# Cross-shaped window attention: x loaded by transposing DMAs, and VectorE's share of the exponentials made from bit fields

## The chip, the cores and the metric

One Trainium2 chip; the program runs on one core. The time is device microseconds of one execution. The kernel before takes 1147.38 us (median of three runs, 1147.14 to 1147.86). The profile comes from another, profiled execution, which took 1150.81 us.

## The reference

`x` is an image of 224 x 224 tokens with 96 channels, bf16. It is projected to q, k and v, each of 96 channels. The first 48 channels attend inside horizontal strips of 8 rows (28 strips of 1792 tokens), the last 48 inside vertical strips of 8 columns (again 28 strips of 1792). Each strip is a full softmax attention of 1792 queries over 1792 keys; the two halves are joined and projected by `wo`.

```python
qkv = jnp.einsum('bhwc,cd->bhwd', x, wqkv)        # C = 96, then q, k, v of 96 channels
scale = C2 ** (-0.5)                              # C2 = 48
# h half: 8 whole rows per strip; v half: 8 whole columns per strip
ah = _softmax(jnp.einsum('bqc,bkc->bqk', qh, kh) * scale, axis=-1)
oh = jnp.einsum('bqk,bkc->bqc', ah, vh)
...
return jnp.einsum('bhwc,cd->bhwd', o, wo)         # o = [oh, ov] along the channels
```

## The kernel before, in words

**Work.** Two strips make a pair (P); 14 horizontal pairs are followed by 14 vertical ones, 28 in all. The two strips of a pair, w = 0 and 1, lie in the two halves of the 128 partitions. A pair has four query chunks (`CH`: 512, 512, 512 and 256 queries). A unit is one key tile of 128 keys against a 512-query chunk, for both strips, or two key tiles against the 256-query chunk: 14 + 14 + 14 + 7 = 49 units per pair, 1372 in all. A unit's scores are 128 x 1024 fp32 in PSUM (two banks).

**Two kinds of unit.** An A unit (`add_a`): QK product on TensorE (L762), exponential on ScalarE from PSUM to a bf16 tile PT (L780), PV product on TensorE (L745) with V_sb as weights. A D unit (`add_d`) has its exponential made by VectorE: L804 scales the scores into an fp16 tile Y_sb; four passes of L814 (J = 4) add a constant each and write int16, whose bits read as bf16 are four shifted piecewise linear powers of two; four PV products (L745 with L_sb and VD_sb) sum them, with V scaled by four weights. GpSimd makes those scaled copies VD_sb (L610). `NDC` says how many units of each chunk are D units: 2, 2, 2 and 1, so 7 of 49.

**Preparation of a pair** (`prep`): x is loaded with tokens in partitions (x_sb, L422); TensorE transposes it against an identity (L538, four groups per pair) and VectorE copies the result from PSUM to xT_sb, channels in partitions (L526, L532); then come the K projection (four groups) with VectorE's copy and row sum (L565) and GpSimd's subtraction of the mean key (L576), the Q projection (four groups, copied by VectorE at L561), and V (four groups, L597, copied at L602). TensorE does such a group in a borrowed PSUM bank; I call it a fill. The results of a chunk leave PSUM at L709, are multiplied by `wo` (L637, L666; seven or eight more fills per pair), divided by the softmax sum (L625, L644, L673) and, in the vertical half, added on GpSimd (L677) and stored (L686).

**What sets the order.** The kernel has its own planner. Each operation is given an engine, a cost, its dependencies and the buffers it takes; the planner simulates the engines and writes out one fixed order per engine. On the chip each engine runs that order, with semaphore waits, whatever its real times are. Preparation of pair P+1 is spread over pair P by `pace`; loads of pair P+2 are put in SP's stream during pair P. PSUM holds a ring of three double banks for scores and fills, and two banks for outputs. All DMAs, loads of x and stores of the result, go through SP's one queue.

Of the kernel before, what the change touches and what calls it, by code (L numbers as in the profile page):

```python
# [8 lines left out]
FP16 = mybir.dt.float16  # L9
FP32 = mybir.dt.float32  # L10
I16 = mybir.dt.int16
# [9 lines left out]
J = 4  # L21


def _bf16(v):
    import struct
    u = struct.unpack("<I", struct.pack("<f", v))[0]
    u = (u + ((u >> 16) & 1) + 0x7FFF) & 0xFFFF0000
    return struct.unpack("<f", struct.pack("<I", u))[0]


def _spline():
    def lin(z):
        n = int(z // 1)
        return (1 + z - n) * 2.0 ** n
    a = [2.0 ** (-j / J) / J for j in range(J)]
    r = [sum(a[j] * lin(i / 4096 + j / J) for j in range(J)) / 2 ** (i / 4096) for i in range(4096)]
    mid = (max(r) + min(r)) / 2
    w = [_bf16(v) for v in a]
    return w, [-log2(J * v * mid) for v in w]


SPL_W, SPL_S = _spline()
Y_MIN = -16000.0


NDC = [2, 2, 2, 1]
DKT = 2
# [198 lines left out]
def bass_standalone__window_attn_cswin__vision_kernel(  # L246
# [19 lines left out]
    TH, FTH = 112, 8  # L266
    RPF = FTH * TH // W
# [3 lines left out]
    NPT, NY, NL, NR = 8, 2, 3, 4  # L271

    es = ExitStack()
    with es:
# [5 lines left out]
        ident = sb("ident", [128, 128], BF16)  # L280
        ident_f = sb("ident_f", [128, 128], FP32)
# [3 lines left out]
        x_sb = [sb(f"x_sb{i}", [128, 2, 16, C], BF16) for i in range(2)]  # L285
# [4 lines left out]
        VD_sb = [sb(f"VD_sb{i}", [128, J, 2, DKT, CP], BF16) for i in range(2)]  # L290
        PT = [sb(f"PT{i}", [128, 1024], BF16) for i in range(NPT)]
        Y_sb = [sb(f"Y_sb{i}", [128, 1024], FP16) for i in range(NY)]
        L_sb = [sb(f"L_sb{i}", [128, J, 1024], I16) for i in range(NL)]
# [21 lines left out]
        s_x = [[[sem(f"s_x{b}{w}{hf}") for hf in range(2)] for w in range(2)] for b in range(2)]  # L315
# [70 lines left out]
        for v in range(2):  # L386
            for w in range(2):
                o_wov0 = first("dve", 0.15, lambda e, v=v, w=w: e.memset(wo_sb[v][w][:], 0.0))
        o_one = first("dve", 0.1, lambda e: e.memset(one_sb[:], 1.0))
        o_iota = first("pool", 0.3, lambda e: e.iota(ident_f[:], [[1, 128]], base=0, channel_multiplier=-1,  # L390
                                                     allow_small_or_imprecise_dtypes=True))
        o_ident = first("dve", 0.2, lambda e: e.tensor_single_scalar(ident[:], ident_f[:], 0.0, ALU.is_equal), [o_iota])
# [8 lines left out]
        x_flat = x[0].rearrange("h w c -> (h w) c")  # L401
        x_vtiles = x[0].rearrange("(kt hh) (j dw) c -> j kt hh dw c", hh=16, dw=8)
# [4 lines left out]
        t_pe = {P: [] for P in range(NP)}  # L407

        def load(P, stream):
            b = P % 2  # L410
            for w in range(2):
                src = x_flat[(2 * P + w) * NTOK:(2 * P + w + 1) * NTOK, :].rearrange("(k p) c -> p k c", p=TH) if is_h[P] else None
                for hf in range(2):
                    sm = s_x[b][w][hf]
                    own = x_tot.get((b, w, hf), 0)
                    if is_h[P]:
                        todo = [(x_sb[b][0:TH, w, hf * FTH:(hf + 1) * FTH, :], src[:, hf * FTH:(hf + 1) * FTH, :])]
                    else:
                        todo = [(x_sb[b][:, w, kt, :], x_vtiles[2 * (P - NPH) + w, kt])
                                for kt in range(8 * hf, min(NKT, 8 * hf + 8))]  # L420
                    for i, (dst, s_) in enumerate(todo):
                        op = Op("sp", 0.06, 2.2, lambda e, dst=dst, s_=s_: e.dma_start(dst, s_),  # L422
                                t_pe[P - 2] if P >= 2 and i == 0 else [], dma=(sm, own if i == 0 else 0))
                        stream.append(op)
                        x_op[(P, w, hf)] = op
                        x_tot[(b, w, hf)] = x_tot.get((b, w, hf), 0) + 16

        load(0, q_first["sp"])
        op_w0 = Op("sp", 0.7, 2.8, lambda e: e.dma_start(w_sb[0:64, :, 0:C2], wqkv.rearrange("c (s d) -> c s d", s=6)[0:64]), [o_w0], dma=(s_w0, 0))
        q_first["sp"].insert(1, op_w0)  # L430
        op_w0 = Op("sp", 0.7, 2.8, lambda e: e.dma_start(w_sb[96:128, :, 0:C2], wqkv.rearrange("c (s d) -> c s d", s=6)[64:96]), [o_w0], dma=(s_w0, 0))
        q_first["sp"].insert(2, op_w0)
# [30 lines left out]
        for P in range(NP):  # L463
            for c in range(NCH):
                k = Chunk()
                k.P, k.c, k.bank, k.last, k.evac = P, c, None, None, None
                n = NKT if CH[c][1] == 512 else NKT // 2
                k.left = (n - NDC[c]) + J * NDC[c]
                k.begun = False
                chunks[(P, c)] = k  # L470
        q_ready, k_ready, v_ready, vd_ready = {}, {}, {}, {}
# [32 lines left out]
        def prep(P, pace=None, startup=False):  # L504
# [7 lines left out]
            xt_w = {}  # L512
            qk_war = last_qk[prev2] if prev2 >= 0 else []
            pv_war = last_pv[prev2] if prev2 >= 0 else []
            xt_war = xt_read.get(prev2, [])
            xt_read[P] = []
            for w in range(2):
                for hf in range(2):
                    if is_h[P]:
                        tp, nt = TH, FTH  # L520
                        ks = [hf * FTH + j for j in range(FTH)]

                        def ev_fn(e, bk, op, w=w, hf=hf):
                            src = bk.bitcast(BF16)[:, 0:FTH * TH].rearrange("c (r bc dw) -> c r bc dw", r=RPF, dw=8)
                            dst = xT_sb[b][:, w, :].rearrange("c (bc r dw) -> c r bc dw", r=SW, dw=8)[:, hf * RPF:(hf + 1) * RPF, :, :]
                            return e.tensor_copy(dst, src)  # L526
                    else:
                        ks = list(range(8 * hf, min(NKT, 8 * hf + 8)))
                        tp, nt = 128, len(ks)

                        def ev_fn(e, bk, op, w=w, ks=ks):
                            return e.tensor_copy(xT_sb[b][:, w, ks[0] * 128:(ks[-1] + 1) * 128], bk.bitcast(BF16)[:, 0:len(ks) * 128])  # L532

                    def pe_fn(e, bk, w=w, ks=ks, tp=tp):
                        bkb = bk.bitcast(BF16)
                        for j, k in enumerate(ks):
                            for h in range(2):
                                ins = e.transpose(bkb[64 * h:64 * h + 64, j * tp:(j + 1) * tp], x_sb[b][0:tp, w, k, 32 * h:32 * h + 64],  # L538
                                                  ident[0:tp, 0:tp])
                        return ins  # L540
                    p, ops = fill(0.055 * nt, pe_fn, [x_op[(P, w, hf)], o_ident],
                                  [("dve", 0.07 + nt * tp / 1920, ev_fn, xt_war, True, dve_ev, [], None)], soft() + xt_war)
                    t_pe[P].append(p)
                    xt_w.setdefault(w, []).append(ops[0])
            xt_all = xt_w[0] + xt_w[1]
            prevk = []
            for kind in "kq":
                for c, (q0, qs) in enumerate(CH):
                    def pe_fn(e, bk, kind=kind, q0=q0, qs=qs):
                        for w in range(2):  # L550
                            ins = e.matmul(bk[64 * w:64 * w + 64, 0:qs], lhsT=w_sb[:, wblk(P, kind), :],  # L551
                                           rhs=xT_sb[b][:, w, q0:q0 + qs], start=True, stop=True)
                        return ins
                    if kind == "q":
                        if startup:
                            def ev_fn(e, bk, op, q0=q0, qs=qs):
                                return e.activation(QT_sb[b][:, q0:q0 + qs], bk[:, 0:qs], ACTF.Copy)
                            evs = [("act", 0.55, ev_fn, qk_war, True, q_first["act"], [], None)]
                        else:
                            def ev_fn(e, bk, op, q0=q0, qs=qs):  # L560
                                return e.tensor_copy(QT_sb[b][:, q0:q0 + qs], bk[:, 0:qs])  # L561
# [20 lines left out]
                    if kind == "q":  # L582
                        q_ready[(P, c)] = ops[0]
                    else:
                        prevk.append(ops[0])
                        if c == NCH - 1:
                            k_ready[P] = ops[-1]
            v_evs = []
            for w in range(2):
                for k0 in range(0, NKT, VS):  # L590
                    n = min(VS, NKT - k0)

                    def pe_fn(e, bk, w=w, k0=k0, n=n):
                        for j in range(n):
                            for h in range(2):
                                t0 = (k0 + j) * 128 + 64 * h
                                ins = e.matmul(bk[64 * h:64 * h + 64, j * C2:(j + 1) * C2], lhsT=xT_sb[b][:, w, t0:t0 + 64],  # L597
                                               rhs=w_sb[:, wblk(P, "v"), 0:C2], start=True, stop=True)
# [4 lines left out]
                    p, ops = fill(0.045 * n, pe_fn, xt_w[w] + [op_w0, o_v1],  # L603
# [4 lines left out]
            vd_ready[P] = []  # L608
            for j in range(J):
                op = Op("pool", 0.1 + 0.001 * 2 * DKT * CP, 0.15 + 0.001 * 2 * DKT * CP, lambda e, j=j: e.tensor_scalar(  # L610
                    VD_sb[b][:, j, :, :, :], V_sb[b][:, :, 0:DKT, :], SPL_W[j], 1.0, ALU.mult, ALU.mult), v_evs + pv_war)
# [308 lines left out]
```

## Time and profile before

| quantity | value | where |
|---|---|---|
| median of three runs | 1147.38 us | times |
| the profiled execution | 1150.81 us | times |
| its span, first to last instruction | 1149.0 us | page |
| outside the span | 1.8 us | difference |
| first exponential of the main loop starts | 14.93 us | timeline, ACT |
| last one ends | 1140.8 us | timeline, ACT |
| busy: PE, ACT, DVE, POOL | 1109.8, 1094.7, 977.8, 198.3 us | page |
| granted TensorE clock, whole span | 0.991 | cores |

A row of a group reads: line, engine, operation, output tile <- input tiles, shapes, count, then busy time and mean duration of one, then the idle time of that engine just ahead of these instructions and what ended it. Busy times of successive instructions that overlap are counted once, so 1176 exponentials of 1085 ns on average are 1091.2 us busy. A row of the timeline merges neighbours of one kind: start, length, count. PE's ends are modelled, so that its busy time overstates how full it is.

### The profile page before, as it was taken

The page shows a single profiled execution, that of the slowest core. Times are in us where ns is not written, and L with a number is a line of the kernel's source. Part 1 is how long each engine was busy: PE and PEld are TensorE (multiplying, and loading weights), DVE is VectorE, ACT ScalarE, POOL GpSimd, SP SyncE. Part 2 cuts the span into 40 slices and gives each one's busy share as a digit, 9 for nine tenths or more (in the row PEclk, how much of TensorE's full clock was granted, in tenths as well). Part 3 has the DMA queues.
Part 4 walks back from the last instruction along what each step waited for, and adds up shares of the span by engine and source line. Part 5 has one row for each costly group of instructions (what it writes and reads, how often), then busy time and mean ns, then how long its engine had stood idle before and what let it go on. Part 6 is the DMA issues. An engine that isn't in the chain of part 4 may idle for free.

```text
span 1149.0 us, 30551 instructions
## 1 busy us (share of the span) xinstructions
PE 1109.8 (97%) x12888; PEld 459.3 (40%) x12888; DVE 977.8 (85%) x2138; ACT 1094.7 (95%) x1182; POOL 198.3 (17%) x256
## 2 busy tenths in 40 slices
PE   8999999999999999999999999999999999999996
PEld 3434433443443344344434433433443443344342
DVE  6898888798888978888888888898889988988974
ACT  5999999999999999999999999999999999999997
POOL 0101010010101001010112222222222313222121
PEclk7999999999999999999999999999999999999998
DMA  4011011101100110110111221121122212210011
GB/s 87 15 25 26 4 23 25 26 2 25 26 18 10 26 26 2 25 22 12 19 30 29 38 35 32 36 38 35 32 37 37 36 32 38 36 31 19 19 20 24
DMA packets 164977, 31.00 MB, mean 27 GB/s; under 512 B 164840, under 2 KB 164840, under 8 KB 164840
## 3 DMA queue, kind: packets, MB, share of 16 engines
q1 hardware_dynamic: 164840, 29.05, 13.8%
q8 instruction: 101, 1.65, 0.6%
q14 instruction: 36, 0.29, 0.1%
HBM read 19.36 MB, written 9.63 MB: 25 GB/s over the span
## 4 chain that ended last, share of the span: by engine, by line
PE 53%; DVE 25%; ACT 19%; issue 2%; DMA 0%; SPq 0%; ACTq 0%; POOL 0%; POOLq 0%
PE ps L745 24%; PE ps L762 19%; ACT PT L780 19%; DVE L_sb L814 10%; DVE Y_sb L804 7%; PE ps L538 4%; PE ps L551 3%; DVE OT_sb L709 2%; DVE KT_sb L565 2%; DVE tmp L673 2%; PE ps L597 2%; PE ps L637 1%; DVE QT_sb L561 1%; DVE V_sb L602 1%; PE ps L666 1%
## 5 line engine op out<-in xcount | busy, mean ns | idle before, releaser
L780 ACT ACTIVATE PT<-ps 128x1024 bf16<-128x1024 f32 x1176 | 1091.2, 1085 | 36.1 <-PE ps L762 26.1
L762 PE MATMUL ps<-QT_sb,KT_sb 48*128 48x512 bf16 (+1 forms) x3136 | 458.2, 357 | 8.5 <-DVE V_sb L602 1.7
L745 PE MATMUL ps<-PT,V_sb 128*64 128x512 bf16 (+1 forms) x2688 | 388.3, 360 | 0.7 <-ACT PT L780 0.7
L814 DVE TENSOR_SCALAR L_sb<-Y_sb 128x1024 int16<-128x1024 f16 x784 | 351.1, 486 | 0.7
L804 DVE TENSOR_SCALAR Y_sb<-ps 128x1024 f16<-128x1024 f32 x196 | 239.2, 1221 | 60.2 <-PE ps L762 58.2
L745 PE MATMUL ps<-L_sb,VD_sb 128*64 128x512 bf16 (+1 forms) x1792 | 270.8, 363 | 18.0 <-DVE L_sb L814 15.1
L762 PEld LDWEIGHTS ps<-QT_sb,KT_sb 48*128 48x128 bf16 x3136 | 122.0, 93 | 292.9 <-ACT PT L780 175.5
L745 PEld LDWEIGHTS ps<-PT,V_sb 128*64 128x64 bf16 x2688 | 126.9, 109 | 127.0 <-issue 104.0
L677 POOL TENSOR_TENSOR out_sb<-tmp,Ph_sb 128x384 bf16<-128x384 f32 (+1 forms) x112 | 95.5, 863 | 341.8 <-DVE tmp L673 286.5
L745 PEld LDWEIGHTS ps<-L_sb,VD_sb 128*64 128x64 bf16 x1792 | 85.5, 108 | 135.8 <-DVE L_sb L814 75.5
L576 POOL TENSOR_SCALAR KT_sb<-KT_sb,negmean 128x1792 bf16<-128x1792 bf16 x27 | 51.2, 1895 | 342.0 <-DVE rc L625 114.2
L610 POOL TENSOR_SCALAR VD_sb<-V_sb 128x256 bf16<-128x256 bf16 x112 | 51.4, 459 | 261.3 <-DVE V_sb L602 254.6
L709 DVE CAST OT_sb<-ps 128x512 bf16<-128x512 f32 x112 | 69.0, 616 | 28.7 <-PE ps L745 28.5
L551 PE MATMUL ps<-xT_sb,w_sb 128*64 128x512 bf16 x448 | 81.3, 374 | 1.1 <-DVE xT_sb L526 0.7
L565 DVE TENSOR_SCALAR_CACHE_REDUCE KT_sb<-ps 128x512 bf16<-128x512 f32 x112 | 67.7, 617 | 8.1 <-PE ps L551 7.7
L561 DVE CAST QT_sb<-ps 128x512 bf16<-128x512 f32 x108 | 66.4, 614 | 4.6 <-PE ps L551 4.6
L538 PE MATMUL ps<-ident,x_sb 112*64 112x112 bf16 (+1 forms) x1680 | 63.3, 219 | 2.4 <-DMA x_sb<-in_x_dram 1.1
L602 DVE CAST V_sb<-ps 128x480 bf16<-128x480 f32 x112 | 55.4, 500 | 10.7 <-PE ps L597 10.0
L538 PEld LDWEIGHTS ps<-ident,x_sb 112*64 112x64 bf16 (+1 forms) x1680 | 50.8, 111 | 28.1 <-issue 24.8
L673 DVE TENSOR_TENSOR tmp<-ps,rc 128x384 f32<-128x384 f32 (+1 forms) x112 | 56.3, 502 | 2.1 <-DVE rc L625 0.2
L625 DVE RECIPROCAL rc<-ps 128x4 f32<-128x4 f32 (+1 forms) x210 | 36.2, 172 | 23.2 <-PE ps L666 11.8
L644 DVE TENSOR_TENSOR Ph_sb<-ps,rc 128x384 bf16<-128x384 f32 x98 | 54.2, 553 | 1.9
(31 smaller groups left out, 315.0 us busy)
## 6 DMA issues: line engine op xcount, KB each, us to landing
x_sb<-in_x_dram SPq DMA_DIRECT2D x56, 168.0 KB, 3.5
x_sb<-in_x_dram SPq DMA_DIRECT2D x392, 24.0 KB, 2.2
out_dram<-out_sb SPq DMA_DIRECT2D x392, 24.0 KB, 1.9
wo_sb<-in_wo_dram SPq DMA_DIRECT2D x4, 9.0 KB
wo_sb<-one_sb SPq DMA_DIRECT2D x4, 0.0 KB
w_sb<-in_wqkv_dram SPq DMA_DIRECT2D x1, 36.0 KB, 2.5
w_sb<-in_wqkv_dram SPq DMA_DIRECT2D x1, 18.0 KB, 2.3
```

The costliest lines, as they stand in the source:

```text
L538: ins = e.transpose(bkb[64 * h:64 * h + 64, j * tp:(j + 1) * tp], x_sb[b][0:tp, w, k, 32 * h:32 * h + 64], ident[0:tp, 0:tp])
L551: ins = e.matmul(bk[64 * w:64 * w + 64, 0:qs], lhsT=w_sb[:, wblk(P, kind), :], rhs=xT_sb[b][:, w, q0:q0 + qs], start=True, stop=True)
L561: return e.tensor_copy(QT_sb[b][:, q0:q0 + qs], bk[:, 0:qs])
L565: return e.tensor_scalar(KT_sb[b][:, q0:q0 + qs], bk[:, 0:qs], 1.0, None, ALU.mult, ALU.add, accum_out=ksum[b][:, c:c + 1])
L673: return e.tensor_tensor(tmp[op.tok["t"]][:, 0:n, :], bk[:, 0:n * (C + 1)].rearrange("p (s c) -> p s c", s=n)[:, :, 0:C], r[:, 0:n].unsque ...
L677: return e.tensor_tensor(out_sb[b][:, w, g[0]:g[0] + n, :], tmp[hold[1].tok["t"]][:, 0:n, :], Ph_sb[:, g[0]:g[0] + n, j, :], ALU.add)
L709: return e.tensor_copy(OT_sb[b][:, q0:q0 + qs], bk[:, 0:qs])
L745: ins = e.matmul(bank(k.bank)[64 * w:64 * w + 64, 0:qs], lhsT=lhs(w, kt), rhs=rhs(w, i, qs), start=(op.tok["first"] and i == 0), stop=(k.l ...
L762: ins = e.matmul(bank(2 * s + w)[:, i * qs:(i + 1) * qs], lhsT=KT_sb[b][64 * w:64 * w + C2, kt * 128:(kt + 1) * 128], rhs=QT_sb[b][64 * w: ...
L780: a.fn = lambda e: e.activation(PT[a.tok["p"]][:].rearrange("p (s n) -> p s n", s=2), two(q.tok["s"]), ACTF.Exp, scale=scale)
L804: d.fn = lambda e: e.tensor_scalar(Y_sb[d.tok["y"]][:, :].rearrange("p (s n) -> p s n", s=2), two(q.tok["s"]), A128, Y_MIN, ALU.mult, ALU.max)
L814: t.fn = lambda e, j=j: e.tensor_scalar(L_sb[hold["l"].tok["l"]][:, j, :], Y_sb[d.tok["y"]][:, :], 127.0 * 128.0 + 128.0 * SPL_S[j], None, ...
```

## The change

1. **x.** The tile x_sb, the identity, the TensorE transposes and VectorE's copies of them go. xT_sb is written by DMA transposes on SP: each reads n tokens of 128 channels (96 and the first 32 of the next token; rows 96 to 127 of the result are not used) and writes 128 x n. A horizontal strip is one such DMA of 1792 tokens, a vertical strip eight of 224, one for each column. The last tokens of the image are loaded by a plain DMA in 2-byte pieces (two DMAs of 96 x 16 elements in all). Tokens of a strip now lie in row order (or column order for vertical strips); keys and values stay in that order, and Q is put back into the old order by VectorE's copy, which now writes with a stride, in four pieces of 448. All chunks of a pair wait for the last of the four. wqkv is loaded by one DMA ahead of the first x.
2. **VectorE's exponential.** Q carries the factor `A128`, so that PSUM holds scores in units of 1/128 of a power of two (ScalarE undoes it with `scale=LN128`). A D unit adds a constant and clamps, PSUM to int16 (I_sb). Two bitwise passes over I_sb make U_sb (mantissa bits under a fixed exponent) and E_sb (exponent bits, a power of two); one product of two tensors, I_sb and U_sb read as bf16, makes G_sb. Two PV products, of E_sb and of G_sb, both with V_sb, take the place of four. GpSimd's scaled copies go.
3. **Shares.** `NDC` is 2, 2, 2, 2: eight units of 49 are D units. Four L-type buffers in place of three. `pace` spreads 12 fills over the pair in place of 16.

In the built programs, ScalarE has 1148 exponentials (1176 before), SP's queue 252 transposing DMAs in place of 448 loads of x, and GpSimd no scaled copies.

```diff
-NDC = [2, 2, 2, 1]
-DKT = 2
+NDC = [2, 2, 2, 2]
...
-                    if is_h[P]:
-                        todo = [(x_sb[b][0:TH, w, hf * FTH:(hf + 1) * FTH, :], src[:, hf * FTH:(hf + 1) * FTH, :])]
...
+                runs = [(j * NTOK, 1, NTOK, 0)] if is_h[P] else [(j * SW + dw, W, H, dw * H) for dw in range(SW)]
...
+                    todo.append((True, xT_sb[b][:, w:w + 1, at:at + n], rows(t0, step, n, 128)))
+                for i, (tr, dst, s_) in enumerate(todo):
+                    fn = (lambda e, dst=dst, s_=s_: e.dma_start_transpose(dst, s_)) if tr else \
+                         (lambda e, dst=dst, s_=s_: e.dma_start(dst, s_, allow_slow_non_contiguous=True))
+                    op = Op("sp", 0.06, 4.0, fn, xt_read.get(P - 2, []) if i == 0 else [], dma=(s_x[b][w], own if i == 0 else 0))
...
-                        for j, k in enumerate(ks):
-                            for h in range(2):
-                                ins = e.transpose(bkb[64 * h:64 * h + 64, j * tp:(j + 1) * tp], x_sb[b][0:tp, w, k, 32 * h:32 * h + 64],
-                                                  ident[0:tp, 0:tp])
...
+                                    dst = QT_sb[b][:, :].rearrange("p (bc r dw) -> p r bc dw", r=SW, dw=8)[:, r * c:r * c + r]
+                                    src = bk[:, 0:QC].rearrange("p (r bc dw) -> p r bc dw", r=r, dw=8)
...
+                                    dst = QT_sb[b][:, :].rearrange("p (h dw) -> p dw h", dw=SW)[:, d * c:d * c + d]
+                                    src = bk[:, 0:QC].rearrange("p (dw h) -> p dw h", dw=d)
+                                return e.tensor_scalar(dst, src, A128, None, ALU.mult)
...
-            d.fn = lambda e: e.tensor_scalar(Y_sb[d.tok["y"]][:, :].rearrange("p (s n) -> p s n", s=2), two(q.tok["s"]),
-                                             A128, Y_MIN, ALU.mult, ALU.max)
+            d.fn = lambda e: e.tensor_scalar(I_sb[d.tok["y"]][:, :].rearrange("p (s n) -> p s n", s=2), two(q.tok["s"]),
+                                             128.0 * ONE, 0.0, ALU.add, ALU.max)
...
-            for j in range(J):
-                t = Op("dve", 0.334, 0.415, None, [d], [], [(ls, "l", 1)] if j == 0 else [])
...
+            f = Op("dve", 0.334, 0.415, None, [d])
+            f.fn = lambda e: e.tensor_scalar(U_sb[d.tok["y"]][:, :], I_sb[d.tok["y"]][:, :], M_FRAC, HALF, ALU.bitwise_and, ALU.bitwise_or)
+            x2 = Op("dve", 0.334, 0.415, None, [d], [], [(ls, "l", 1)])
+            x2.fn = lambda e: e.tensor_scalar(E_sb[x2.tok["l"]][:, :], I_sb[d.tok["y"]][:, :], M_EXP, E_LOW, ALU.bitwise_and, ALU.bitwise_or)
+            g = Op("dve", 0.60, 0.68, None, [f, x2], [], [], lambda op: ys.free(d.tok["y"], [op]))
+            g.fn = lambda e: e.tensor_tensor(G_sb[x2.tok["l"]][:, :], I_sb[d.tok["y"]][:, :].bitcast(BF16), U_sb[d.tok["y"]][:, :].bitcast(BF16), ALU.mult)
+            dve_ts.extend([f, x2, g])
+            for t, buf in ((x2, E_sb), (g, G_sb)):
...
-                prep(P + 1, pace=lambda n, base=base: [act_of[base + int(n * NA * PACE / 16)]])
+                prep(P + 1, pace=lambda n, base=base: [act_of[base + int(n * NA * PACE / 12)]])
```

## The prediction

> **What bounds the kernel now.** I read the split of the span by windows first: before the first exponential, the main loop, and after the last.
>
> ```profile
> 0.00:14.93 14.93, 11.46 (x148) 5.88 (x148) 8.87 (x31) 3.45 (x7) 0.44 (x5) 0.78 0.60 111
> 14.93:1140.80 1125.87, 1097.36 (x12730) 452.90 (x12728) 967.55 (x2102) 1091.15 (x1176) 196.77 (x249) 1.00 0.14 26
> 1140.80:1149.00 8.20, 0.95 (x12) 0.49 (x12) 1.38 (x5) 0.07 (x1) 1.05 (x2) 0.55 0.19 36
> ```
>
> Columns: stretch, its us, then busy us of PE, PEld, DVE, ACT and POOL, granted clock, DMA share, GB/s. The main loop is 1125.87 of 1149.0 us and ScalarE is busy in 1091.15 of it. PE looks as full, but its ends are modelled, so the waits decide:
>
> ```profile
> POOL out_sb L677 <- DVE tmp L673: 286.5, 58, 9.9
> ...
> PEld ps L762 <- ACT PT L780: 175.5, 517, 0.6
> ...
> PEld ps L745 <- DVE L_sb L814: 75.5, 209, 1.2
> ...
> ACT PT L780 <- PE ps L762: 26.1, 60, 1.4
> ```
>
> Columns: total us, times, longest. The weight loads of QK stand still 175.5 us because ScalarE has not freed a score buffer; ScalarE waits for QK 26.1 us. So ScalarE paces the loop, and PE, DVE and the fixed order only open gaps in it. ScalarE's pace and the gaps are in its own timeline (start, length, count):
>
> ```profile
> 350.52 3.77 ACT L780 ACTIVATE PT<-ps 128x1024 bf16<-128x1024 f32 x4 [0.49 <-PE ps L762]
> ...
> 754.91 1.02 ACT L780 ACTIVATE PT<-ps 128x1024 bf16<-128x1024 f32 x1 [0.81 <-PE ps L762]
> 756.17 1.94 ACT L780 ACTIVATE PT<-ps 128x1024 bf16<-128x1024 f32 x2 [0.24 <-PE ps L762]
> ```
>
> Four in a row take 3.77 us and a single one 1.02, so one follows another after (3.77 - 1.02) / 3 = 0.917 us. 1176 x 0.917 = 1078.4 us; the loop's other 47.5 us are gaps like the 0.81 and 0.24 shown, 1.7 us per pair. So the execution is 14.9 (head) + 1078.4 + 47.5 + 8.2 (tail) + 1.8 (outside the span) = 1150.8. That profiled execution is 3.4 us above the median.
>
> The rows the change touches, from the groups by line (busy us, mean ns | idle before):
>
> ```profile
> L780 ACT ACTIVATE PT<-ps 128x1024 bf16<-128x1024 f32 x1176 | 1091.2, 1085 | 36.1 <-PE ps L762 26.1 <-PE ps L745 8.8
> L814 DVE TENSOR_SCALAR L_sb<-Y_sb 128x1024 int16<-128x1024 f16 x784 | 351.1, 486 | 0.7
> L804 DVE TENSOR_SCALAR Y_sb<-ps 128x1024 f16<-128x1024 f32 x196 | 239.2, 1221 | 60.2 <-PE ps L762 58.2
> ...
> L526 DVE COPY xT_sb<-ps 128x896 bf16<-128x896 bf16 x56 | 34.1, 619 | 15.3 <-PE ps L538 15.2
> L532 DVE COPY xT_sb<-ps 128x1024 bf16<-128x1024 bf16 x28 | 19.1, 681 | 0.0
> L532 DVE COPY xT_sb<-ps 128x768 bf16<-128x768 bf16 x28 | 15.5, 553 | 8.7 <-PE ps L538 8.7
> ```
>
> **ScalarE.** One unit of 49 leaves it in every pair: 28 x 0.917 = 25.7 us, all on the path. 1148 x 0.917 = 1052.7 us. The other factor in `scale` costs nothing: same instruction, same shapes.
>
> **TensorE.** The transposes go: 63.3 us busy (L538, 1680 in the page). D's PV products fall from 28 x 7 x 4 = 784 unit passes to 28 x 8 x 2 = 448; at 270.8 / 784 = 0.345 us that is -116.1. A's PV loses one unit of 42: 388.3 / 42 = -9.2. QK is the same. PE's busy time goes from 1109.8 to 921 us, a factor of 0.83. PE is not the bound, so this shows only in the gaps. Fills per pair fall from 12 + 4 + 7.5 = 23.5 to 19.5, again 0.83. I let the gaps shrink by both: 47.5 x 0.83 x 0.83 = 32.7 us. Ends: 10 us (nearly all were collisions with fills and D's PV) and 47.5 (VectorE's chain or the fixed order makes them, not PE's load).
>
> **VectorE.** Out: 351.1 + 239.2 + 34.1 + 19.1 + 15.5 = 659.0, which leaves 977.8 - 659.0 = 318.8 us. In: 224 passes PSUM to int16, shape and sides as L804, at 239.2 / 196 = 1.22: 273.3 us. Then 448 bitwise passes and 224 products, which the trace does not have. A bitwise pass has one 2-byte source and a 2-byte result in SBUF, like L814: 351.1 / 784 = 0.448 us. Its other end is one element per cycle, L804's 1.22. I take 0.448, same shape and same kind of instruction: 200.7 us. The product of two bf16 tiles lies between the same ends; nearest is the 2-byte copy of 1024 elements that does not reach L814's rate, 0.681 (L532): 152.5 us. Sum: 318.8 + 273.3 + 200.7 + 152.5 = 945.3 us, or 86% of a span of about 1108, against 85% now. So VectorE stays beside ScalarE, at nothing. The cover is 15% wide: a product at 1.22 adds 121 us (96%), bitwise passes at 1.22 add 346 (over the span).
>
> The Trainium skill ("VectorE: DVE Perf Modes", "The perf-mode tier table") gives a product of two 16-bit tiles half the rate of a one-source pass; this fits the value taken, and the sum by it is the same.
>
> The copy of Q writes with a stride now, 1792 elements per pair as before (66.4 us, L561). L526 already writes 2-byte runs of 8 with gaps, 896 elements in 0.619 us, without a loss against L532's dense 1024 in 0.681. I cost it at nothing; if every strided write took twice as long it would be 66 us on VectorE, 92% full. All chunks of a pair wait for its last Q piece. That is the eighth of 12 paced fills, at about 0.9 x 8/12 = 0.6 of the pair ahead, some 15 us early: nothing.
>
> **GpSimd.** 51.4 us of VD_sb go; D's PV then waits for V itself. GpSimd is 17% busy, so nothing.
>
> **The load of x.** Before, the first K product starts at 9.19 us: x lands at 4.7 to 7.9, then transposes and copies. After, it starts when both strips of pair 0 have landed, and pair 1's first K product stands in PE's order right behind the first four QK products (two units), waiting for pair 1's strips, with all QK queued behind it. Let t be a strip's time through SP and the DMA engines; wqkv is issued first, at about 1.4 us for 0.67. K then starts near 2.1 + 2t + 2, the 2 being a landing (2.2 us in the page). The near row: half a strip by plain rows is one DMA, and seven took 5.25 us of SP's queue, 0.75 each, landing after 3.5. So t is at least 1.5 and K starts near 7 to 8.6. The far row: the queue's 164840 packets took 13.8% of 16 engines' 1149 us, 15.4 ns each; if every 32-byte piece (16 tokens of one channel) cost a packet, a strip is 14336 x 15.4 / 16 = 13.8 us. Then K starts at 31.7 instead of 9.2 (+22.5), and pair 1's strips land near 59 while PE reaches that product near 38 (+21): +44 us. After that a pair needs 27.6 us of DMA in a pair of some 39, loaded a pair ahead: hidden. I take the near row: with t = 2.5 K starts at 9.1, head unchanged. In the steady state SP issues at most 16 transposes per pair where it issues 28 loads now (28 in 18.7 us), behind the same waits; stores queue behind them as they do behind loads. The 2-byte DMA (1536 pieces, 1.5 us at 15.4 ns over 16 engines) is prefetched too. Tail: unchanged, 8.2.
>
> One rule speaks against this part. "VectorE: DVE Perf Modes", "The three transpose paths", gives 390 ns for a 128 x 128 transpose on TensorE and 1309 ns by DMA. This trace has only the TensorE side (63.3 us busy for 28 x 28 squares, 81 ns each); no run here shows the DMA's. If 1309 ns held for each of a strip's 14 squares in turn, t would be 18.3 us, an estimate from that page, and the sum about 1107 + 62.
>
> **Sum.** 14.9 + 1052.7 + 32.7 + 8.2 + 1.8 = 1110.3 for a profiled execution; less 3.4: 1107 us.
>
> **Rivals.**
> (a) The gaps stay, or VectorE becomes co-critical. For it: DVE waits for QK 58.2 us already and D's PV waits for L814 75.5 us; E and G must come in time, and an order written for one cost stalls in sequence if a pass is longer. Against: two PV passes wait per D unit instead of four. Gaps of 47.5 give 1122; a product at 1.22 makes VectorE 1067 us busy, and with about 70 us of unavoidable waiting (its 60.2 at L804 and the ends) 1137.
> (b) The gaps nearly vanish: 10 us give 1084.
> (c) Transposing DMAs are slow: t = 13.8 gives 1107 + 44 = 1151; from a t of 18 to 19 (two strips per pair of 39 us) every pair would wait too.
> (d) The slower one: bitwise passes at one element per cycle. VectorE is then 1291 us busy, the bound; with the head before its first D pass (15 us) about 1305, slower by 14%. It decides once bitwise passes and products average over (1085 - 318.8 - 273.3) / 672 = 0.73 us, 1085 being the loop as forecast; I took 0.53. For it: no bitwise pass is in the trace. Against: L814's integer result did not slow it.
>
> **Chances.** Forecast, 1095 to 1118: 0.50. (a), to 1145: 0.17. (b): 0.09. (c): 0.13, of which 0.03 ends within 0.2% of 1147.4 (what a measurement of this kernel can tell from no change) and 0.10 above. (d): 0.11. Faster 0.76, same 0.03, slower 0.21. The range 1082 to 1151 takes in all but (d), the upper part of (c), and a little of (b).
>
> **What would show it.** Right: 1148 exponentials with runs at 0.917, gaps near 33 us, first exponential near 15 us; E and U passes near 0.45 us and G near 0.68; VectorE about 945 us busy; PE near 921. Wrong: PE waiting for DMA xT_sb in the first 60 us or in every pair; bitwise passes of 1.2 us; ScalarE waiting for PV or QK more often than now while PE waits for G_sb.

## The result, and the profile after

The changed kernel takes 1210.11 us (median of four runs, 1207.2 to 1217.32) beside 1147.62 us for the kernel before on the same chip: ratio 1.0553, 95% interval [1.0503, 1.0602]. It is slower by 62 us where 1107 was forecast. The profiled execution took 1211.87 us, its span 1210.1.

The rows of the groups by line that answer to those shown of before:

```profile
L736 ACT ACTIVATE PT<-ps 128x1024 bf16<-128x1024 f32 x1148 | 1071.0, 1092 | 117.3 <-PE ps L718 115.4
L760 DVE TENSOR_SCALAR I_sb<-ps 128x1024 int16<-128x1024 f32 x224 | 276.0, 1232 | 47.9 <-PE ps L718 44.1
L770 DVE TENSOR_TENSOR G_sb<-I_sb,U_sb 128x1024 bf16<-128x1024 bf16 x224 | 182.0, 812 | 3.0
L521 DVE TENSOR_SCALAR QT_sb<-ps 128x448 bf16<-128x448 f32 x108 | 151.5, 1423 | 37.0 <-PE ps L504 37.0
L766 DVE TENSOR_SCALAR U_sb<-I_sb 128x1024 int16<-128x1024 int16 x224 | 97.6, 436 | 2.4
L768 DVE TENSOR_SCALAR E_sb<-I_sb 128x1024 int16<-128x1024 int16 x224 | 92.6, 413 | 0.0
```

ScalarE's own work is as forecast: 1148 exponentials. What is new stands behind the second bar: 115.4 us of waiting for QK (L718), where it was 26.1. The new exponential's passes are near their forecasts, its product (0.812 us for 0.68) less so. One row is far off: the copy of Q, 1.423 us on average where 0.62 was taken. A mean over two forms hides the size, so next comes the spread of that line's instructions (minimum, median, maximum in ns):

```profile
L521 DVE TENSOR_SCALAR QT_sb<-ps x108: 611/2130/2366, 32.3 to 1141.6; 128x448 bf16<-128x448 f32 x108
```

The 52 copies of horizontal pairs, which write runs of 8 elements, take 0.62 us each; the 56 of vertical pairs, which write single elements 16 bytes apart, take 2.13 to 2.37, 2.17 on average. The windows of one horizontal pair and two vertical ones (columns as before: us, busy PE, PEld, DVE, ACT, POOL, clock, DMA share, GB/s) show where the time is:

```profile
300.00:338.00 38.00, 36.73 (x376) 13.84 (x375) 33.57 (x69) 37.79 (x42) 2.17 (x1) 1.00 0.16 26
791.80:837.80 46.00, 39.19 (x378) 13.91 (x374) 41.06 (x70) 38.67 (x42) 9.34 (x10) 0.93 0.18 35
742.30:791.80 49.50, 45.68 (x378) 15.81 (x372) 39.44 (x72) 38.90 (x42) 8.83 (x10) 0.76 0.19 36
```

A horizontal pair takes 38.0 us, with ScalarE busy in 37.8 of it. A vertical pair, which differs by GpSimd's additions and the stores, takes 44.0 to 49.5 us, VectorE busy 6 to 7.5 us longer and the TensorE clock below full. None of these engines is full in such a pair, so the loss is in the order. The timeline of after inside one of them:

```profile
712.77 1.02 POOL L633 TENSOR_TENSOR out_sb<-tmp,Ph_sb 128x384 bf16<-128x384 f32 x1 [5.96 <-DVE tmp L629]
713.06 1.28 DVE L770 TENSOR_TENSOR G_sb<-I_sb,U_sb 128x1024 bf16<-128x1024 bf16 x1
...
714.35 4.14 DVE L521 TENSOR_SCALAR QT_sb<-ps 128x448 bf16<-128x448 f32 x2
...
716.56 0.36 PE L622 MATMUL ps<-wo_sb,OT_sb 128*64 128x97 bf16 x8 [0.70 <-DVE QT_sb L521]
716.85 0.39 PE L718 MATMUL ps<-QT_sb,KT_sb 48*128 48x512 bf16 x2
717.29 1.02 ACT L736 ACTIVATE PT<-ps 128x1024 bf16<-128x1024 f32 x1 [1.99 <-PE ps L718]
718.12 0.37 DVE L581 RECIPROCAL rc<-ps 128x4 f32<-128x4 f32 x1
718.55 0.61 PE L718 MATMUL ps<-QT_sb,KT_sb 48*128 48x512 bf16 x2 [1.30 <-DVE rc L581]
```

Two copies of Q hold VectorE for 4.14 us. The output product L622 needs the PSUM bank that the first of them empties; QK (L718) stands behind L622 in TensorE's fixed order, and ScalarE starves for 1.99 us. The next stop is 1.30 us, for a reciprocal that sat behind the second copy. Over the whole kernel TensorE's weight loads wait 49.7 us for this copy (total us, times, longest):

```profile
PEld ps L504 <- DVE QT_sb L521: 20.1, 13, 1.8
PEld ps L718 <- DVE QT_sb L521: 19.8, 24, 1.7
...
PEld ps L622 <- DVE QT_sb L521: 9.8, 6, 1.9
```

### The profile page after: what moved, and what is told of

Read it like the earlier page. It is cut to its first block, busy times and chain, and to the rows that moved or that the text cites. A ratio compares the mean times of both kernels' runs of the same rounds, so it can differ in the third digit from the quotient of the medians.

```text
span 1210.1 us, 24996 instructions
## 1 busy us (share of the span) xinstructions
PE 1096.9 (91%) x10424; PEld 399.7 (33%) x10424; DVE 1033.1 (85%) x1941; ACT 1074.4 (89%) x1154; POOL 156.2 (13%) x143
## 4 chain that ended last, share of the span: by engine, by line
DVE 39%; ACT 31%; PE 26%; issue 3%; POOL 1%; DMA 0%; POOLq 0%; SPq 0%
ACT PT L736 31%; PE ps L701 11%; PE ps L718 11%; DVE I_sb L760 11%; DVE QT_sb L521 9%; DVE G_sb L770 6%; DVE E_sb L768 3%; DVE U_sb L766 2%; DVE KT_sb L525 2%; DVE OT_sb L665 2%; DVE tmp L629 1%; PE ps L504 1%; PE ps L593 1%; PE ps L560 1%; DVE rc L581 1%
## 5 line engine op out<-in xcount | busy, mean ns | idle before, releaser
L736 ACT ACTIVATE PT<-ps 128x1024 bf16<-128x1024 f32 x1148 | 1071.0, 1092 | 117.3 <-PE ps L718 115.4
L718 PE MATMUL ps<-QT_sb,KT_sb 48*128 48x512 bf16 (+1 forms) x3136 | 512.0, 374 | 63.2 <-ACT PT L736 16.8
L701 PE MATMUL ps<-PT,V_sb 128*64 128x512 bf16 (+1 forms) x2576 | 467.4, 387 | 0.8 <-ACT PT L736 0.3
L760 DVE TENSOR_SCALAR I_sb<-ps 128x1024 int16<-128x1024 f32 x224 | 276.0, 1232 | 47.9 <-PE ps L718 44.1
L718 PEld LDWEIGHTS ps<-QT_sb,KT_sb 48*128 48x128 bf16 x3136 | 127.2, 94 | 388.9 <-ACT PT L736 184.4
L770 DVE TENSOR_TENSOR G_sb<-I_sb,U_sb 128x1024 bf16<-128x1024 bf16 x224 | 182.0, 812 | 3.0
L521 DVE TENSOR_SCALAR QT_sb<-ps 128x448 bf16<-128x448 f32 x108 | 151.5, 1423 | 37.0 <-PE ps L504 37.0
L504 PE MATMUL ps<-xT_sb,w_sb 96*64 96x512 bf16 (+1 forms) x448 | 86.2, 387 | 19.9 <-DVE QT_sb L521 14.9
L766 DVE TENSOR_SCALAR U_sb<-I_sb 128x1024 int16<-128x1024 int16 x224 | 97.6, 436 | 2.4
L701 PE MATMUL ps<-G_sb,V_sb 128*64 128x512 bf16 (+1 forms) x560 | 94.3, 367 | 5.4 <-DVE G_sb L770 4.9
L701 PE MATMUL ps<-E_sb,V_sb 128*64 128x512 bf16 (+1 forms) x560 | 93.9, 365 | 0.5 <-DVE E_sb L768 0.3
L768 DVE TENSOR_SCALAR E_sb<-I_sb 128x1024 int16<-128x1024 int16 x224 | 92.6, 413 | 0.0
L622 PE MATMUL ps<-wo_sb,OT_sb 128*64 128x97 bf16 x784 | 38.3, 222 | 14.4 <-DVE QT_sb L521 7.5
```

The lines of the kernel that those rows point to most:

```text
L504: ins = e.matmul(bk[64 * w:64 * w + 64, 0:qs], lhsT=w_sb[0:C, wblk(P, kind), :], rhs=rhs, start=True, stop=True)
L521: return e.tensor_scalar(dst, src, A128, None, ALU.mult)
L701: ins = e.matmul(bank(k.bank)[64 * w:64 * w + 64, 0:qs], lhsT=lhs(w, kt), rhs=rhs(w, i, qs), start=(op.tok["first"] and i == 0), stop=(k.l ...
L718: ins = e.matmul(bank(2 * s + w)[:, i * qs:(i + 1) * qs], lhsT=KT_sb[b][64 * w:64 * w + C2, kt * 128:(kt + 1) * 128], rhs=QT_sb[b][64 * w: ...
L736: a.fn = lambda e: e.activation(PT[a.tok["p"]][:].rearrange("p (s n) -> p s n", s=2), two(q.tok["s"]), ACTF.Exp, scale=LN128)
L760: d.fn = lambda e: e.tensor_scalar(I_sb[d.tok["y"]][:, :].rearrange("p (s n) -> p s n", s=2), two(q.tok["s"]), 128.0 * ONE, 0.0, ALU.add, ...
```

## The experiments

Theory 1: the single 2-byte writes of the vertical copy of Q are the loss. Theory 2: eight units in 49 overload VectorE beside GpSimd's additions in the vertical half. Theory 3: the short transposing DMAs of vertical pairs are the loss.

**Dense write.** All kernels are given as edits of the changed one. This one leaves the reordering of Q out, so it is no repair. (The copies in question are 56; the 52 below is the number of the horizontal ones.)

```diff
-    dst = QT_sb[b][:, :].rearrange("p (h dw) -> p dw h", dw=SW)[:, d * c:d * c + d]
+    dst = QT_sb[b][:, QC * c:QC * c + QC].rearrange("p (dw h) -> p dw h", dw=d)
```

> Vertical pairs: VectorE's copy of Q writes dense, so Q and with it the result stay in column order (the reordering is left out); every instruction and every order is as in the changed kernel, only these 52 destinations differ. Theory 1 (the 2-byte writes at a step of 16 bytes cost VectorE 2.15 us instead of 0.62, and the fixed order turns that into gaps on ScalarE and a colder TensorE): the copy takes about 0.62, vertical pairs fall from some 46 to 38-39 us, the granted clock of the second half returns to 1.00, the span is about 1095 to 1105 us. Theory 2 (eight units in 49 overload VectorE beside GpSimd's adds in the vertical half): the span falls only by the 52 x 1.5 = 80 us of copies at most, and gaps of several us per pair stay, 1140 or more. Theory 3 (the eight short transposing DMAs per strip hold up the vertical half): no change, about 1205.

Measured: 1108.66 us (one run). The groups by line:

```profile
L736 ACT ACTIVATE PT<-ps 128x1024 bf16<-128x1024 f32 x1148 | 1061.0, 1098 | 24.3 <-PE ps L718 23.5
L521 DVE TENSOR_SCALAR QT_sb<-ps 128x448 bf16<-128x448 f32 x108 | 66.3, 618 | 27.2 <-PE ps L504 26.9
```

Same instructions, order and waits; the copies cost 66.3 us, the figure the prediction used, and ScalarE's wait for QK falls from 115.4 to 23.5. Theory 1 stands. Theory 2 falls: with the same eight units the time is far below its 1140.

**Reordering inside TensorE's operand.** The Q projection reads its moving operand in the final order; VectorE copies densely.

```diff
+    rhs = xT_sb[b][0:C, w, :].rearrange("c (dw h) -> c h dw", dw=SW)[:, q0 // 8:(q0 + qs) // 8, :]
...
+    return e.tensor_scalar(QT_sb[b][:, q0:q0 + qs], bk[:, 0:qs], A128, None, ALU.mult)
```

> Vertical pairs: the Q projection itself reads x in the old order, its moving operand stepping 224 elements between neighbours, in chunks of 512 and 256; VectorE then copies dense. Theory 1: about 1095 to 1110 us if TensorE reads with that step at full rate; if it takes four times as long (some 1.2 us more per group of two products, four groups in each of 14 pairs) PE still has the room, and it stays below 1125. Theories 2 and 3: 1140 or more, 1205.

Measured: 1114.74 us, ratio to before 0.9713 [0.9698, 0.9727]. The stride costs TensorE instead: the two 512-wide products of a Q group take 1.02 to 1.04 us together, where those of K, whose operand is dense, take 0.38 to 0.41. Vertical pairs take 39.5 us.

**Reordering on the reading side.** The same elements, with the stride where VectorE reads PSUM; the operand keeps runs of 64, the write is dense.

```diff
+    rhs = xT_sb[b][0:C, w, :].rearrange("c (dw h) -> c dw h", dw=SW)[:, :, q0 // 8:(q0 + qs) // 8]
...
+    return e.tensor_scalar(QT_sb[b][:, q0:q0 + qs].rearrange("p (h dw) -> p h dw", dw=SW),
+                           bk[:, 0:qs].rearrange("p (dw h) -> p h dw", dw=SW), A128, None, ALU.mult)
```

> Vertical pairs: the Q projection reads runs of 64 tokens of each of the eight columns, and VectorE's copy reads PSUM with a step of 64 fp32 elements and writes dense. Theory 1 in its narrow form (it is the stepped write that is slow): the copy takes about 0.68 for 512 elements and the kernel about 1095 to 1105 us. If any stepping of a two-dimensional pattern is slow, the copy takes over 2 us here too and the kernel stays above 1190.

Measured: 1104.19 us, ratio 0.9629 [0.9607, 0.9651]. It computes all of the reference, so it is the change's gain without the stride's price. Vertical pairs take about 37.75 us, but two take 43.9 and 44.3; I call such pairs late pairs, and they come up again below.

**One DMA per strip.** A vertical pair loads 1792 consecutive tokens by one transposing DMA; gathering the columns is left out, so the tokens are the wrong ones. The strided write stays.

```diff
-    runs = [...] if is_h[P] else [(j * SW + dw, W, H, dw * H) for dw in range(SW)]
+    runs = [(j * NTOK, 1, NTOK, 0)]
```

> Vertical pairs load 1792 consecutive tokens by one transposing DMA per strip, as horizontal pairs do (wrong tokens: the gathering of columns is left out); Q's stepped copy stays. Theory 3: vertical pairs fall to 38-40 us, span about 1100. Theories 1 and 2: within 10 us of the changed kernel, 1200 to 1215.

Measured: 1207.58 us (one run), vertical pairs 44 to 48 us. Theory 3 falls.

**The price by itself.** A program with nothing but VectorE's copies (and two forms on ScalarE), six of each.

> Computes nothing of the reference (it writes zeros): VectorE alone, six copies of 448 elements each, one after the other, on a line for each form; ScalarE afterwards with two forms. Theory 1 (the price is that of a 2-byte write alone in its 16 bytes, on VectorE, whatever else runs): dense 0.6 to 0.7 us, runs of 8 the same, the changed kernel's vertical form 2.1 to 2.2 us, bf16 at a step of 8, 16 and 32 elements 2.1 to 2.2 as well, step 2 and 4 somewhere between; from SBUF instead of PSUM the same price as from PSUM. Rival A (the price comes from what runs beside it in the kernel, GpSimd or the DMAs): the vertical form 0.6 to 0.8 here. Rival B (the price is that of reading PSUM in two halves, not of the write): step 8 with a plain read stays at 0.6 to 0.7. Open between sub-theories: fp32 at a step of 16 bytes is 0.6 if only writes of under 4 bytes pay, 2.1 if any write alone in its 16 bytes pays; pairs (4 bytes at a 16-byte step) cost half of the single ones, 1.1, if the price is one write slot per 16 bytes touched.

Measured, in the groups by line (L93 is ScalarE, one bf16 every 16 bytes; L58 VectorE the same; L52 the changed kernel's vertical form; L56 one bf16 every 8 bytes, L54 every 4; L64 two neighbours every 16 bytes; L74 a strided read of PSUM with a dense write; L48 dense on both sides; L50 runs of 8):

```profile
L93 ACT ACTIVATE d<-ps 128x448 bf16<-128x448 f32 x6 | 12.9, 2148 | 0.2
L58 DVE TENSOR_SCALAR d<-ps 128x448 bf16<-128x448 f32 x6 | 12.8, 2136 | 0.2
L52 DVE TENSOR_SCALAR d<-ps 128x448 bf16<-128x448 f32 x6 | 12.8, 2136 | 0.2
...
L56 DVE TENSOR_SCALAR d<-ps 128x448 bf16<-128x448 f32 x6 | 6.9, 1148 | 0.2
...
L54 DVE TENSOR_SCALAR d<-ps 128x448 bf16<-128x448 f32 x6 | 3.9, 656 | 0.2
L64 DVE TENSOR_SCALAR d<-ps 128x448 bf16<-128x448 f32 x6 | 3.7, 624 | 0.2
L74 DVE TENSOR_SCALAR d<-ps 128x448 bf16<-128x448 f32 x6 | 3.7, 624 | 0.2
L48 DVE TENSOR_SCALAR d<-ps 128x448 bf16<-128x448 f32 x6 | 3.7, 624 | 0.2
L50 DVE TENSOR_SCALAR d<-ps 128x448 bf16<-128x448 f32 x6 | 3.7, 624 | 0.2
```

With nothing beside it the vertical form costs 2.136 us against 0.624 for the dense copy and for runs of 8, so the price is its own and rivals A and B fall. It grows with the step: 0.656 at 4 bytes, 1.148 at 8, 2.136 at 16, 2.025 and 2.099 at 32 and 64. Two neighbours every 16 bytes cost nothing, not the 1.1 that one sub-theory gave. One fp32 every 16 bytes takes 0.942 (dense fp32 was not measured). That the source matters was not expected (one bf16 every 16 bytes from SBUF takes 1.157, whether the source is fp32 or bf16); why is open.

**The strided write in every second vertical pair** (even P), the strided read in the others.

> The strided write in every second vertical pair only (28 of 56 copies), the strided read in the others; all else as in the changed kernel. Theory 1 (each strided write's own stall, plus what the halved TensorE clock adds after it): the pairs with it 44 to 48 us, the others about 38, total near the middle, 1155 to 1160. Rival (a backlog that carries from pair to pair, so that one dense pair in two lets VectorE catch up): the pairs with it under 42, total under 1130.

Measured: 1144.18 us (one run). The windows of four vertical pairs in turn:

```profile
593.00:640.00 47.00, 40.42 (x376) 14.05 (x374) 41.03 (x70) 38.75 (x42) 9.31 (x10) 0.89 0.18 36
640.00:677.80 37.80, 36.84 (x381) 13.48 (x376) 34.04 (x71) 37.78 (x42) 8.90 (x10) 1.00 0.22 41
677.80:722.50 44.70, 40.60 (x378) 14.41 (x373) 39.21 (x72) 38.25 (x42) 8.78 (x10) 0.89 0.20 39
722.50:760.40 37.90, 36.45 (x376) 13.59 (x374) 34.51 (x70) 37.71 (x42) 9.14 (x10) 1.00 0.21 41
```

A pair during which the strided copies of the next one run takes 43.2 to 47.0 us, seven pairs in all; the pair after it takes 37.7 to 38.1, as VectorE is then rid of them. The rival falls: these pairs are not under 42. But such a pair takes 45.3 us on average, against 46.4 in the changed kernel, where they follow one another; why is not shown. This is one reason why the total is below the 1155 expected; the other is that the expectation took the middle to a version with two late pairs, and here there are none (see the next run for what makes them).

**The loops of the copy exchanged.** The repair that the probe suggests.

```diff
-    dst = QT_sb[b][:, :].rearrange("p (h dw) -> p dw h", dw=SW)[:, d * c:d * c + d]
-    src = bk[:, 0:QC].rearrange("p (dw h) -> p dw h", dw=d)
+    dst = QT_sb[b][:, :].rearrange("p (h dw) -> p h dw", dw=SW)[:, :, d * c:d * c + d]
+    src = bk[:, 0:QC].rearrange("p (dw h) -> p h dw", dw=d)
```

> The changed kernel with the two loops of the vertical copy of Q exchanged: the two columns of a copy run innermost, so that it writes two neighbouring elements (4 bytes) every 16 bytes; same instructions, same data, nothing else. Theory 1 (the price is that of a 2-byte write without a neighbour; the probe gave 0.62 us for this form alone): 0.62 us per copy in the kernel, vertical pairs 37.7 but for those in which x comes late; 1102 to 1107, as with the strided read. Rival (in the kernel, beside other work, the spaced write costs more than alone): copies over 1 us, 1120 or more.

Measured: 1105.31 us (median of five runs), ratio 0.9633 [0.9608, 0.9658]; 0.62 us per copy. The weight loads' wait for this copy falls from 49.7 to 9.6 us. Theory 1 is shown a second way. Two late pairs again (41.1 and 43.9 us). SyncE's timeline from one vertical pair, and TensorE's at the later late pair:

```profile
749.19 21.26 SPq L397 DMA_TRANSPOSE xT_sb<-in_x_dram  x16
770.50 17.15 SPq L642 DMA_DIRECT2D out_dram<-out_sb  x24
787.76 3.75 SPq L397 DMA_TRANSPOSE xT_sb<-in_x_dram  x3
791.55 2.51 SPq L642 DMA_DIRECT2D out_dram<-out_sb  x4
```

```profile
976.67 0.64 PE L504 MATMUL ps<-xT_sb,w_sb 96*64 96x512 bf16 x2 [3.44 <-issue]
```

The queue never rests: transposes for 21.3 us, 24 to 28 stores for 17 to 19, so about 40.5 us per pair, while a pair lasts 38. Each load is 2 to 3 us later than the last, until the first K product waits 3.44 us. The profile names no releaser there ("issue"), but the last transpose of that pair is issued at 974.1 us and lands at 976.6, and the product starts at 976.67. Then the clock is at half (0.50 from 977.0 to 980.5, 0.92 over that pair), and the pair takes 6 us more.

**Half of the stores on GpSimd**, on top of the strided read (odd `kt`, with semaphores of their own; GpSimd's additions now wait for all earlier stores of their buffer, not only the last):

```diff
+    on = "pool" if kt % 2 else "sp"
```

> The strided read, and every second store of the output issued by GpSimd instead of SyncE. Theory (in the version with the strided read two vertical pairs take 44 us because SyncE needs 41 us per pair to issue 16 transposes and 28 stores while a pair takes 37.75, so that x comes later from pair to pair until the first K product waits and the TensorE clock halves): with 14 stores fewer SyncE needs about 31 us per pair, no pair over 39, total 1104.2 minus 12 = 1092, 1089 to 1096. Rival (GpSimd's issuing holds up VectorE's passes, or the dips come from something else): 1100 or more, dips stay.

Measured: 1103.41 us, ratio 0.9616 [0.96, 0.9632]. The late pairs are gone in the profiled execution (clock 0.996), as the theory said, but the time hardly moves, where 1089 to 1096 was expected: the other vertical pairs go from 37.75 to 38.30 us and the tail from 8.1 to 12.6 us, so issuing on GpSimd has a price, as the rival said; by which wait it slows the pairs is not shown. It is no test of SyncE's share alone; the next is.

**One transposing DMA per strip, loops exchanged** (again the wrong tokens in vertical pairs, so gathering is left out):

> As the run with the exchanged loops, but a vertical pair loads 1792 consecutive tokens of x per strip by one transposing DMA instead of eight (the wrong tokens, so that gathering the columns is left out): 2 transposes and 28 stores per pair on SyncE, some 24 us of issuing instead of 41. Theory (the two late pairs are SyncE's queue running late by 3.3 us per pair): no pair over 39 in the vertical half, TensorE clock near 1.0, 1104 minus 12.7 = 1089 to 1093. Rival (the late pairs come from elsewhere): they stay, 1102 to 1106.

Measured: 1095.43 us (one run), clock 0.996, no vertical pair over 38.5 us but the last, which takes about 40 us in the other versions too. The late pairs come from SyncE's queue, and they cost 10 us, somewhat less than the 12.7 expected. This run and the one above with one DMA per strip differ in the loops of the copy alone: 1207.58 against 1095.43. So where x is never late the strided write costs 112 us (one run each).

**Seven and nine units**, loops exchanged (`NDC` 2, 2, 2, 1 and 3, 2, 2, 2):

> As the run with the exchanged loops, but seven units in 49 on VectorE as before the change: 1176 exponentials on ScalarE. Theory (ScalarE bounds every pair): 28 x 0.917 = 26 us more than eight units, 1128 to 1132; what is left to the 1147.6 of before, 16 to 20, is then what the x by DMA and the cheaper exponential give through shorter gaps. Rival (VectorE and TensorE bound): 1104 to 1110, no worse than eight.

> As the run with the exchanged loops, but nine units in 49 on VectorE: 1120 exponentials. With half of the stores on GpSimd nine units gave 1093.9 against 1103.4, 9.5 less instead of 26. Theory (VectorE and ScalarE are near balance at nine): 9 to 14 less than eight, 1090 to 1096, with pairs of 37.0 to 38.5 whose idle time stands at ScalarE behind QK^T. Rival (it was GpSimd's DMA issuing that took VectorE's time): 26 less, 1078 to 1082.

Measured: 1123.96 us, ratio 0.9784 [0.9767, 0.9801], and 1098.88 us, 0.9566 [0.9545, 0.9587]. The eighth unit is worth 18.7 us, less than the 26 expected: at seven units pairs last 39.1 us and none is late, at eight two are; without the late pairs it would be 28.5 (1123.96 - 1095.43). The ninth gives 6.4 more in place of 9 to 14: VectorE is 92% busy, and late pairs of 43.5 and 42.6 us are back.

**Nine units with half of the stores on GpSimd and the strided read:**

> As the run with half of the stores on GpSimd, but nine units in 49 on VectorE (one more per pair), so ScalarE has 1120 exponentials instead of 1148: 28 x 0.917 = 26 us less if ScalarE still bounds every pair. VectorE gains 28 x (1.22 + 0.85 + 0.75) = 79 us, about 34.0 + 2.8 = 36.9 us per pair beside ScalarE's 36.7: theory (VectorE becomes the bound at about nine units) 1085 to 1105, no real gain over eight; rival (ScalarE still bounds) 1066 to 1070.

Measured: 1093.92 us, ratio 0.9532 [0.9515, 0.9548]: in the theory's range, though it expected no real gain over eight units and this is 9.5 us. This is the fastest version that computes the reference.

## Why the prediction was wrong

**The step that failed:** "The copy of Q writes with a stride now ... I cost it at nothing; if every strided write took twice as long it would be 66 us on VectorE". The near row was L526, runs of 8 elements with gaps, which cost nothing. The vertical copy writes runs of one. Its 56 copies cost 2.17 us each, 3.5 times a dense one: 151.5 - 66.4 = 85 us more on VectorE. Without this the changed kernel takes 1105.31 us (e5_pairs), 1104.19 (e3_read_strided) or 1108.66 (e1_dense_q), against the 1107 forecast. That the rest of the sum comes so near is in part luck: the late pairs, which it did not foresee, cost 10 us, and the other gaps closed further than it said, to 17.1 us in place of 32.7 (see below). Two errors lie in the step. The row taken as near shares the word "stride" and not the run length; the two forms of one line needed two prices. And the 66 us of the other end were left beside ScalarE as cover ("92% full"; the sum gives 91) and out of the range, whose slower end came from rivals (c) and (d); neither took place. The 85 us cost 105 (1210.11 - 1105.31), and 112 without the late pairs, which the slow kernel does not have: VectorE was not full, but a copy of 2 us, or two in a row, holds a PSUM bank that TensorE's fixed order needs next. 15% of idle time is no cover for a single long instruction. Rival (a) had named the mechanism, "an order written for one cost stalls in sequence if a pass is longer", but had hung it on the product and ended it at 1145.

The Trainium skill has a rule that bears on this: "Advanced Engine Details and Errata", "SBUF Cachelines", says that SBUF has lines of 16 bytes, that it needs at least two hits on a line to absorb the memory's latency, and that the tolerated stride depends on the type. The probe agrees at the 16-byte step (2.136 us) and for two neighbours in a line (0.624). It differs at an 8-byte step, two accesses to a line, which already costs 1.148 us; there the measurement decides.

**The other steps.**
- Head: forecast unchanged; the first exponential is at 15.26 us (14.93 before), with t near 2.1 us per strip on SyncE, so that the estimate of 18.3 us is not borne out. Rival (c) falls.
- Bitwise passes 0.448 us: measured 0.436 and 0.413. Rival (d) falls.
- Product 0.68 us: 0.812. With nothing of GpSimd beside it it takes 0.68 to 0.69 (165 of 224 with the loops exchanged), beside GpSimd's addition up to 1.28, as in the timeline above, and beside its subtraction of the mean key 1.62. On VectorE that is 182.0 in place of 152.5 us; the 30 us more outweigh the 11 that the bitwise passes save. VectorE as a whole: 945 forecast, 952.9 with the loops exchanged.
- TensorE 921 us busy: 1045 with the loops exchanged. The rows count overlapping neighbours once, and fewer overlap now, so scaling a row by its number of passes was wrong: A's PV was 388.3 us for 2688 matmuls of 360 ns on average and is 445.7 for 2576 of 370. The term of the gaps hung on this: its factor 0.83 for TensorE is 1045 / 1109.8 = 0.94.
- Gaps 32.7 us: with the loops exchanged the main loop lasts from 15.08 to 1095.64, 1080.6 - 1052.7 = 27.9 us of gaps; with one DMA per strip 17.1. Seven units: 1099.3 - 1078.4 = 20.9, where before had 47.5. So x by DMA and the cheaper exponential close more gaps than forecast, 23.9 us in time at equal shares (1147.81 - 1123.96), and SyncE gives 10 back. No run tells the two apart, and the rule that gave 32.7 (two factors of 0.83) is not confirmed.
- "SP issues at most 16 transposes per pair where it issues 28 loads now (28 in 18.7 us)": fewer, but not cheaper. 16 transposes take 21 us, and with the stores the queue needs more than a pair lasts: this is where the late pairs come from.

**What stays open.** How the 105 us divide between the stalls themselves and the TensorE clock that falls after them. Of the 13 vertical pairs of after that can be cut out whole, the three with a clock of 0.96 take 44.0 to 44.6 us and those at 0.86 or less 46.0 to 49.5, against 38: most of the loss is there at a nearly full clock. This is a correlation; no run held the clock fixed. Nor did a run tell the planner the true cost: it plans this copy at 0.07 + 448 / 960 = 0.54 us. How much an order written for 2.17 us would win back is open.

## What to carry to other kernels

Price a strided write by its run length and, where the runs are of one element, by its step too (bf16 from PSUM: 0.656 us at 4 bytes, 1.148 at 8, 2.136 at 16). Where a copy must reorder, put the stride on the side that reads PSUM, or let at least two neighbours run innermost. An engine with idle time still delays the others when one instruction grows from 0.6 to 2.1 us, if a fixed order behind it waits for the bank that it empties. When loads change kind, add up the queue's issuing time per pass of the loop, because a queue that is some per cent too slow shows only many passes later.

## What the runs showed of the hardware

- One bf16 written every 16 bytes from PSUM: 2.14 us for 448 elements on VectorE and 2.15 on ScalarE (0.54 dense); from SBUF 1.16; two neighbours every 16 bytes 0.62; one fp32 every 16 bytes 0.94 (p1_probe). Reading PSUM at a step of 64 elements and writing densely costs what a dense copy costs (0.682 us for 512 elements in e3_read_strided, 0.681 before).
- A moving operand that steps 224 elements slows a pair of 512-wide matmuls from 0.38 to 0.41 us to 1.02 to 1.04 (e2_rhs_strided).
- A product of two bf16 tiles of 1024 on VectorE takes 0.68 to 0.69 us, and up to 1.62 with a GpSimd instruction beside it (e5_pairs).
- A transposing DMA holds SyncE's queue for 1.3 us at 224 tokens and 2.1 at 1792; a store holds it for 0.7 (e5_pairs, after). On GpSimd's queue a store takes 0.54 us of GpSimd (e6_pool_stores).
